# Linear attention, soft mixture and a wide layer in one program: weight tiles requested later, slot sums in another bank, and work moved between GpSimd and VectorE

## The chip, the cores and the metric

The program runs on one core of a Trainium2 chip. Times are microseconds on the device, of one execution. The kernel before takes 391.36 us, the median of three runs (391.15 to 392.89).

## The reference

Three layers follow each other. The first is a linear attention with decay, over batch 4, 8 heads, 768 positions and head size 48. A state of 48x48 per head is decayed by `w` at every position and takes up the outer product of key and value; the position's own product counts with the bonus `u` in place of 1:

```
cur = einsum('bhd,bhe->bhde', u * kt, vt)
y[:, :, t] = einsum('bhd,bhde->bhe', rt, state + cur)
state = w * state + einsum('bhd,bhe->bhde', kt, vt)
```

Its 3072x384 output `x` goes into a soft mixture of 8 experts with 4 slots each: `logits = x @ phi`, a softmax over the tokens makes each of the 32 slots' inputs (`d.T @ x`), each expert takes its 4 slots through `relu(s @ w1[e]) @ w2[e]`, and a softmax over the slots mixes the results back to tokens. The third layer is `g = max(0.01*h, h)` of `h = x @ w_in` and `g @ w_out`, with 2048 hidden columns. All is float32.

## The kernel before, in words

The attention is worked in 24 passes, called units in the code (`i`, 0 to 23): 6 chunks of 128 positions (`c`) times 4 pairs of heads (`k`, or `hp`), chunk by chunk. A pass needs two tiles from memory: `rkb` (r and k with the head dimension on the partitions, 128x1024 numbers, 512 KB) and `tk` (v, k and r with the tokens on the partitions, 128x1152, 576 KB). There are five buffers of each. SyncE issues all transfers in program order; in pass `i` it first requests that pass's weight tiles (the list `WST` says which pass each of the 22 tiles is requested in), then `rkb` and `tk` of unit `i+4`, whose buffers come free when TensorE has read those of unit `i-1`.

The order of instructions on every engine is that of the Python code. For one unit the steps are these. `scale` (line 303) multiplies r and k of `rkb` by powers of the decay, two instructions of 112x512: r on GpSimd, k on VectorE. The table of powers lies in SBUF (`ET`) and in PSUM (`ETp`). `bonus` (line 310) multiplies r by u and then by k in the token layout, two instructions of 128x384 on GpSimd (lines 314 and 317; for units 0 and 1 on VectorE). `diag` (line 319) sums that on VectorE into `Dg` and lets ScalarE write eight diagonal blocks into `base` (line 337). `keys` (line 342) scales the keys for the state. `scores` (line 355) are 8 products into the bank `A`; `keep` (line 365) copies their kept triangle from `A` into `base`, two VectorE instructions. `attend` (line 376) multiplies the state (line 391) and the values (line 399) into `Y`; `evac` copies `Y` to `xT` on ScalarE (line 432). `logits` (line 434) multiplies `xT` by phi, `tokens` transposes it, `update` makes the new state (`U`, then `St` on VectorE, line 421).

In pass `i` scale, bonus and diag are done for unit `i+2`, scores and keep for `i+1`, attend and update for `i`, logits and tokens for `i-1`. Once a chunk, one pass after its end (`k == 0`), `soft1` takes the maximum and the exponential of the chunk's logits. In the pass after that (`k == 1`: 5, 9, 13, 17, 21) `soft2` transposes them, `slots` (line 509) multiplies them with the tokens (`pS`), and `slots_add` adds the result to `acc` on VectorE (lines 523 and 526). `pS` has a buffer of the pool `psM`, which has two and which it shares with `U`, the token transposes `px` and the narrowing's `low`; so it takes the buffer that `U` of the same pass had, which is free when VectorE has read it. The logits of a chunk lie in a 2 KB bank of their own (`psL`, one buffer; 128 of its 512 columns are used).

Four of the weight tiles (`wir`, of `w_in`) are 64-bit floats and are narrowed to 32 bits between the passes, half a tile at a time, in the eight passes of the list `NARROW`: ScalarE makes one part one or two passes ahead (`narrow_a`, line 167), VectorE does three instructions of 128x384 at the end of the pass (lines 172, 178, 183). The weight pool `wp` has 18 buffers; tiles 18 to 21 of the list take the buffers of the narrowed tiles 0 to 3. Tiles 4 to 19 are `w1`; 20 and 21 are the first rows tiles of `w2`. The remaining rows of `w2` are requested after the passes, as buffers come free.

After the passes TensorE works nearly without a break: the experts' first product (`ph`, line 751), the second (`po`, line 794), the mixing weights' transposes, and then the wide layer (lines 959 and 1016) to the end.

Of the kernel before, what the change touches and what calls it, by code (L numbers as in the profile page):

```python
# [8 lines left out]
F32 = mybir.dt.float32  # L9
# [4 lines left out]
ALU = mybir.AluOpType  # L14
# [4 lines left out]
C = 128  # L19
NC = S // C  # L20
NP = H // 2
NU = NC * NP
DM = H * D
# [16 lines left out]
FILL_L = {3: 2}  # L40
WST = list(range(22))
NARROW = [5, 7, 9, 11, 13, 15, 17, 19]
WCH = 8
# [74 lines left out]
def chunked(ctx, tc, rk, tok, wT, urep, phi, w1, w2, win, wout, outT, dbg=None, check=False):  # L118
# [184 lines left out]
    def scale(i, eng=nc.gpsimd, part=(0, 1)):  # L303
        for x in part:
            t = rk_t[i][:, x]
            e = ETp[:R] if x and i else ET
            e = e[:, i % NP : i % NP + 1, :].broadcast_to([R, B, C])
            (nc.vector if x else eng).tensor_tensor(t, t, e, op=ALU.mult)  # L308

# [124 lines left out]
    def logits(i):  # L434
        c, hp = divmod(i, NP)
        if hp == 0:
            lw[c] = psL.tile([128, 4, C], F32, name=f"l{c}", tag="l")
            lps[c] = lw[c][:, 0]
        for b in range(B):
            nc.tensor.matmul(  # L440
                lps[c][32 * b : 32 * b + 32, :], phi_sb[:, hp, b % 2, :], xT[i][:, b, :],
                start=hp == 0, stop=hp == NP - 1, skip_group_check=True,
            )
# [65 lines left out]
    def slots(c, pS=None):  # L509
        if pS is None:  # L510
            pS = psM.tile([128, DM], F32, name=f"pS{c}", tag="m")
        for b in range(B):
# [51 lines left out]
    keys(0)  # L564
    powers(2)

    for i in range(NU):
# [15 lines left out]
        if i + 1 < NU:  # L583
            scores(i + 1)
            keep(i + 1)
        if i >= 1:
            logits(i - 1)
        if 2 <= i < NP:
            tokens(i - 2)(nc.scalar.copy)
        if i + 2 < NU:  # L590
            bonus(i + 2)
        attend(i)
        slot = bool(c) and k == 1
        if slot:
# [4 lines left out]
        if i < NP - 1:  # L599
            powers_t(i + 1)  # L600
            keys(i + 1)
        if i == 0:
            powers(3)
        if i == NP:
# [17 lines left out]
        if slot:  # L622
            pS = slots(c - 1)
        if i >= NP - 1:
            tok_copy(nc.scalar.copy)
        if slot:
            slots_add(c - 1, pS)
        if i in NARROW:
# [5 lines left out]
            narrow_d(wi[:, j, w], wirs[j], w, low)  # L634
        ahead = i + 1 + i % 2
        if ahead in NARROW and k > 1:
            j, x = divmod(NARROW.index(ahead), 2)
            w = slice(x * WCW // 2, (x + 1) * WCW // 2)
            narrow_a(wi[:, j, w], wirs[j], w)

    load_w2_unit(NLD - 1)
    m1, s1 = mst[:, NC - 1 : NC], sst[:, NC - 1 : NC]
    cb = cp.tile([128, 8], F32, name="cb")
# [547 lines left out]
```

## Time and profile before

| what | us |
|---|---|
| median of three runs | 391.36 |
| the profiled execution's own time | 391.55 |
| its span, from first to last instruction | 389.8 |
| busy: TensorE, VectorE, ScalarE, GpSimd | 369.3, 272.5, 234.1, 149.6 |
| the passes, to the first instruction of line 751 | 127.3 |

The span is 1.75 us shorter than the execution's own time; the rest lies before the first and after the last instruction. Busy time adds up over stages: for the passes, which end at 127 us, one reads the stretch from 0 to 127, and there what each engine waited for. "DVE" is VectorE, "ACT" ScalarE, "POOL" GpSimd, "PE" TensorE, "SPq" the queue of SyncE. In a row of the timeline the bracket at the end is the idle time of the engine ahead of the instruction and what ended it.

### The profile page before, as it was taken

The numbers are of one execution on the slowest core, as the hardware profiler recorded it, in microseconds if no ns is written. First come the engines' busy times: TensorE is split into PE (matmuls) and PEld (weight loads), VectorE is DVE, ScalarE is ACT, GpSimd is POOL, SyncE is SP. The second block draws the span as 40 slices with busy tenths as digits, with TensorE's granted clock in tenths as the row PEclk, the third lists the DMA queues.
The fourth block names the chain that finished last, engine by engine and source line by source line (L and its number), as shares of the span: only waits on it lengthen the run. The fifth ranks groups of instructions, "written<-read, shape, count | busy, mean of one in ns | idle before, by whom it ended". The sixth has DMA issues, their size and how long they took to land.

```text
span 389.8 us, 8335 instructions
## 1 busy us (share of the span) xinstructions
PE 369.3 (95%) x3162; PEld 282.7 (73%) x3162; DVE 272.5 (70%) x472; ACT 234.1 (60%) x542; POOL 149.6 (38%) x150
## 2 busy tenths in 40 slices
PE   6889898989999999899999999999999999999994
PEld 3567776767776345788888878888888888888883
DVE  6778787878785638667577755777765766586762
ACT  3378686969785214757676648667655455545440
POOL 4798998988641303155423332555200000000000
PEclk9999999999999999999999999999999999999998
DMA  7999999999998899400022220000000120021202
GB/s 250 407 419 414 415 413 418 416 416 417 414 386 297 286 392 419 184 2 0 0 83 82 81 82 0 0 3 1 1 3 0 72 91 0 1 105 59 81 3 88
DMA packets 21090, 70.16 MB, mean 180 GB/s; under 512 B 2240, under 2 KB 7344, under 8 KB 20912
## 3 DMA queue, kind: packets, MB, share of 16 engines
q1 hardware_dynamic: 21040, 69.53, 45.9%
q8 instruction: 27, 0.44, 0.5%
q14 instruction: 23, 0.19, 0.1%
HBM read 64.80 MB, written 4.72 MB: 178 GB/s over the span
## 4 chain that ended last, share of the span: by engine, by line
PE 69%; DVE 12%; ACT 7%; POOL 5%; issue 4%; DVEq 0%; POOLq 0%; ACTq 0%
PE o L1016 51%; PE h L959 6%; ACT base L337 6%; PE po L794 3%; DVE base L368 3%; PE ph L751 3%; DVE Dg L322 2%; DVE rkb L308 2%; POOL rkb L308 2%; POOL tk L314 1%; DVE low L178 1%; PE pS L515 1%; DVE low L172 1%; POOL tk L317 1%; POOL tk L349 1%
## 5 line engine op out<-in xcount | busy, mean ns | idle before, releaser
L973 ACT CAST gh<-t 128x512 fp32r<-128x512 f32 x94 | 58.4, 621 | 69.1 <-DVE t L969 61.5
L969 DVE TENSOR_TENSOR t<-t,h 128x512 f32<-128x512 f32 (+1 forms) x97 | 65.7, 678 | 26.0 <-ACT t L965 25.1
L1016 PE MATMUL o<-gh,woh 128*128 128x512 f32 x279 | 80.4, 395 | 0.0
L1016 PE MATMUL o<-gl,woh 128*128 128x512 f32 x279 | 80.2, 394 | 0.0
L1016 PE MATMUL o<-gh,wol 128*128 128x512 f32 x279 | 80.2, 394 | 0.0
L978 DVE TENSOR_TENSOR gl<-t,gh 128x512 fp32r<-128x512 f32 x71 | 50.2, 708 | 40.7 <-ACT gh L973 39.9
L965 ACT ACTIVATE t<-h 128x512 f32<-128x512 f32 (+1 forms) x97 | 57.4, 593 | 13.7 <-PE h L959 13.1
L1016 PEld LDWEIGHTS o<-gh,woh 128*128 128x128 f32 x279 | 52.5, 188 | 12.3 <-DVE sum L1087 0.2
L1016 PEld LDWEIGHTS o<-gl,woh 128*128 128x128 f32 x279 | 52.5, 188 | 12.1
L1016 PEld LDWEIGHTS o<-gh,wol 128*128 128x128 f32 x279 | 52.3, 188 | 12.0 <-issue 0.4
L337 ACT ACTIVATE base<-anti,Dg 128x128 f32<-128x128 f32 x176 | 53.9, 389 | 11.5 <-DVE Dg L322 10.7
L978 POOL TENSOR_TENSOR gl<-t,gh 128x512 fp32r<-128x512 f32 x23 | 34.2, 1488 | 51.8 <-ACT gh L973 48.5
L368 DVE COPY_PREDICATED base<-mask,A 128x512 f32<-128x512 int32 x48 | 34.2, 735 | 11.1 <-ACT base L337 10.4
L959 PE MATMUL h<-cT,Gs 128*128 128x512 f32 (+1 forms) x97 | 37.7, 394 | 1.4 <-ACT Gs L927 1.4
L360 PE MATMUL A<-rkb 48*128 48x128 f32 x384 | 28.0, 284 | 5.3 <-DVE base L368 4.2
L360 PEld LDWEIGHTS A<-rkb 48*128 48x128 f32 x384 | 23.7, 188 | 11.7 <-issue 3.5
L308 POOL TENSOR_TENSOR rkb<-rkb,ETw 112x512 f32<-112x512 f32 x23 | 27.9, 1212 | 5.2 <-DMA rkb<-in_rk_dram 5.2
L399 PE MATMUL Y<-base,tk 128*48 128x128 f32 x376 | 25.5, 277 | 0.0
L314 POOL TENSOR_TENSOR tk<-tk,u_sb 128x384 f32<-128x384 f32 x22 | 22.1, 1002 | 4.1 <-DMA tk<-in_tok_dram 3.0
L399 PEld LDWEIGHTS Y<-base,tk 128*48 128x48 f32 x376 | 19.4, 122 | 4.9 <-issue 3.0
L317 POOL TENSOR_TENSOR tk<-tk 128x384 f32<-128x384 f32 x22 | 22.1, 1003 | 1.7
L861 POOL TENSOR_TENSOR wol<-wor,woh 128x384 fp32r<-128x384 f32 x8 | 9.5, 1197 | 33.4 <-ACT woh L860 33.4
(199 smaller groups left out, 476.2 us busy)
## 6 DMA issues: line engine op xcount, KB each, us to landing
w<-in_w_dram SPq DMA_DIRECT2D x24, 768.0 KB, 10.9
tk<-in_tok_dram SPq DMA_DIRECT2D x23, 576.0 KB, 9.9
rkb<-in_rk_dram SPq DMA_DIRECT2D x24, 512.0 KB, 9.7
wir<-in_win_dram SPq DMA_DIRECT2D x8, 768.0 KB, 13.5
out_dram<-sum SPq DMA_DIRECT2D x17, 256.0 KB, 2.1
wor<-in_wout_dram SPq DMA_DIRECT2D x4, 768.0 KB, 9.6
wir<-in_wout_dram SPq DMA_DIRECT2D x4, 768.0 KB, 4.2
w2t<-in_w_dram SPq DMA_DIRECT2D x4, 576.0 KB, 6.5
```

The lines of the kernel that those rows point to most:

```text
L308: (nc.vector if x else eng).tensor_tensor(t, t, e, op=ALU.mult)
L314: eng.tensor_tensor(rr, rr, u_sb[:, hp : hp + 1, :].broadcast_to([128, B, 2 * D]), op=ALU.mult)
L337: nc.scalar.activation(base[i][:, h, b, :], anti, AF.Copy, scale=Dg[i][:, h * B + b : h * B + b + 1])
L360: nc.tensor.matmul(a[:, h, b, :], rk_t[i][p0 : p0 + D, 1, b, :], rk_t[i][p0 : p0 + D, 0, b, :], start=True, stop=True,)
L368: nc.vector.copy_predicated(base[i][:, :, 2 * j : 2 * j + 2, :], mask.unsqueeze(1).unsqueeze(1).broadcast_to([128, 2, 2, C]), a[:, :, 2 * ...
L399: nc.tensor.matmul(ys[r][g : g + D, j, :], v[:, b, D * h : D * h + D], base[i][:, h, b, :], start=c == 0, stop=True, skip_group_check=True,)
L959: nc.tensor.matmul(t, Gs[f // 8][:, f % 8 * 128 : f % 8 * 128 + 128], cT[blk // 3][:, blk % 3 * TB + c.start : blk % 3 * TB + c.stop], sta ...
L965: nc.scalar.mul(tt[n][:, c], t, 0.01)
L969: nc.vector.tensor_tensor(tt[n][:, c], tt[n][:, c], h, op=ALU.max)
L973: nc.scalar.copy(gh[n][:, c], tt[n][:, c])
L978: eng.tensor_tensor(gl[n][:, c], tt[n][:, c], gh[n][:, c].bitcast(F32), op=ALU.subtract)
L1016: nc.tensor.matmul(os[m][:, c], w[j][:, k, m * 128 : (m + 1) * 128], g[n][:, c], start=k == 0 and w is woh and g is gh and c.start == 0, s ...
```

## The change

Six edits, all in the passes.

- `WST`: the first weight tile is requested in pass 2 and not in pass 0, one a pass to pass 18, none in pass 19, two each in 20 and 21, and the last after the passes. The last rows and tokens (unit 23) are requested in pass 19; 17 tiles stand ahead of them and 5 behind, before it was 20 and 2.
- `slots` writes into columns 128 to 511 of the bank in which the next chunk's logits stand, and no longer into a buffer of `psM`. The tile of that bank is made in `slots`; the chunk's first logits, `logits(i-1)` of the pass with `k == 1`, move from the middle of the pass to right behind the slots' product.
- `NARROW`: the narrowings of passes 13 and 17 are now in passes 20 and 22. The new table `NARROW_A` says in which pass ScalarE makes its part.
- `SCALE_V`: r of the units 9, 13, 17 and 21 is scaled on VectorE (in passes 7, 11, 15 and 19), from the table in PSUM.
- The bonus of unit 2, in pass 0, is on VectorE.
- `powers(3)`, the table of powers of the last pair of heads (three VectorE and three ScalarE instructions), stands ahead of pass 0 and no longer at its end.

```
-WST = list(range(22))
-NARROW = [5, 7, 9, 11, 13, 15, 17, 19]
+WST = [*range(2, 19), 20, 20, 21, 21, NU]
+NARROW = [5, 7, 9, 11, 15, 19, 20, 22]
+NARROW_A = {3: 5, 6: 7, 7: 9, 10: 11, 14: 15, 18: 19, 19: 20, 21: 22}
+SCALE_V = (9, 13, 17, 21)
...
-            e = ETp[:R] if x and i else ET
+            e = ETp[:R] if (x or i in SCALE_V) and i else ET
...
-            (nc.vector if x else eng).tensor_tensor(t, t, e, op=ALU.mult)
+            (nc.vector if x or i in SCALE_V else eng).tensor_tensor(t, t, e, op=ALU.mult)
...
-            lw[c] = psL.tile([128, 4, C], F32, name=f"l{c}", tag="l")
+            if c == 0:
+                lw[c] = psL.tile([128, 4, C], F32, name=f"l{c}", tag="l")
...
-            pS = psM.tile([128, DM], F32, name=f"pS{c}", tag="m")
+            lw[c + 1] = psL.tile([128, 4, C], F32, name=f"l{c + 1}", tag="l")
+            pS = lw[c + 1][:, 1:4].rearrange("p a t -> p (a t)")
...
     powers(2)
+    powers(3)
...
-        if i >= 1:
+        slot = bool(c) and k == 1
+        if i >= 1 and not slot:
             logits(i - 1)
...
-            bonus(i + 2)
+            bonus(i + 2, nc.gpsimd if i else nc.vector)
...
-        if i == 0:
-            powers(3)
...
         if slot:
             pS = slots(c - 1)
+            logits(i - 1)
...
-        ahead = i + 1 + i % 2
-        if ahead in NARROW and k > 1:
-            j, x = divmod(NARROW.index(ahead), 2)
+        if i in NARROW_A:
+            j, x = divmod(NARROW.index(NARROW_A[i]), 2)
...
     load_w2_unit(NLD - 1)
+    load_weights(len(WST) - 1)
```

What the two programs have on VectorE around pass 0, before and then with the change. `ETw` is the table of powers, `rkb` the scaling of unit 2, `base` the `keep` of unit 1, `tk` the bonus and `Dg` the sum of unit 2; the line numbers of the changed kernel are two to four higher.

```order
L274 SCALAR_TENSOR_TENSOR ETw<-W_139,ETw,zp 112x63
L308 TENSOR_TENSOR rkb_111<-rkb_111,ETp 112x512
L368 COPY_PREDICATED base_197<-mask,A_213 128x2x256 x2
L274 SCALAR_TENSOR_TENSOR ETw<-W_139,zp 112x64
L286 RECIPROCAL ETw<-ETw 112x1
L274 SCALAR_TENSOR_TENSOR ETw<-W_139,ETw,zp 112x63
L322 TENSOR_REDUCE Dg_247<-tk_131 128x4x2
L419 COPY St<-U_258 112x192
```

```order
L276 SCALAR_TENSOR_TENSOR ETw<-W_139,ETw,zp 112x63
L276 SCALAR_TENSOR_TENSOR ETw<-W_139,zp 112x64
L288 RECIPROCAL ETw<-ETw 112x1
L276 SCALAR_TENSOR_TENSOR ETw<-W_139,ETw,zp 112x63
L310 TENSOR_TENSOR rkb_111<-rkb_111,ETp 112x512
L370 COPY_PREDICATED base_197<-mask,A_217 128x2x256 x2
L316 TENSOR_TENSOR tk_131<-tk_131,u_sb 128x384
L319 TENSOR_TENSOR tk_131<-tk_131 128x384
L324 TENSOR_REDUCE Dg_245<-tk_131 128x4x2
L421 COPY St<-U_256 112x192
```

The three instructions of `powers(3)` moved ahead of the scaling, and the two of the bonus, which GpSimd had, came in ahead of the sum.

VectorE in passes 13 to 15, before and then with the change: `acc` adds the slots' sums, `low` and `wi` are the narrowing, `rkb` the scaling of units 15, 16 and 17, `base` the `keep`.

```order
L421 SCALAR_TENSOR_TENSOR St<-St,W_139,U_1233 112x192
L526 SCALAR_TENSOR_TENSOR acc<-acc,st_1138,pS_1248 128x384
L528 SCALAR_TENSOR_TENSOR sst<-sst,st_1138 128x1
L172 TENSOR_SCALAR low_1259<-wir_328 128x384
L178 SCALAR_TENSOR_TENSOR low_1259<-wi,low_1259 128x384
L183 SCALAR_TENSOR_TENSOR wi<-wir_328,low_1259 128x384
L308 TENSOR_TENSOR rkb_110<-rkb_110,ETp 112x512
L368 COPY_PREDICATED base_1223<-mask,A_1270 128x2x256 x2
L322 TENSOR_REDUCE Dg_1305<-tk_1096 128x4x2
L421 SCALAR_TENSOR_TENSOR St<-St,W_139,U_1317 112x192
L308 TENSOR_TENSOR rkb_111<-rkb_111,ETp 112x512
L368 COPY_PREDICATED base_1307<-mask,A_1341 128x2x256 x2
```

```order
L423 SCALAR_TENSOR_TENSOR St<-St,W_139,U_1221 112x192
L530 SCALAR_TENSOR_TENSOR acc<-acc,st_1131,l_1236 128x384
L532 SCALAR_TENSOR_TENSOR sst<-sst,st_1131 128x1
L310 TENSOR_TENSOR rkb_110<-rkb_110,ETp 112x512
L370 COPY_PREDICATED base_1211<-mask,A_1258 128x2x256 x2
L324 TENSOR_REDUCE Dg_1293<-tk_1089 128x4x2
L423 SCALAR_TENSOR_TENSOR St<-St,W_139,U_1305 112x192
L310 TENSOR_TENSOR rkb_111<-rkb_111,ETp 112x512 x2
L370 COPY_PREDICATED base_1295<-mask,A_1329 128x2x256 x2
```

The narrowing of pass 13 is gone from behind `acc`, and in pass 15 the scaling is two instructions in place of one.

TensorE in pass 17, before and then with the change: `A` the scores of unit 18, then 19, `l` the logits, `Y` the attention and the transposes of `soft2`, `pS` the slots' sums, which are `l` from columns 128 on with the change; the state's products `U` are left out.

```order
L360 MATMUL A_1495<-rkb_112 128x128 x8
L440 MATMUL l_1506<-xT_1449,phi_sb 32x128 x4
L391 MATMUL Y<-rkb_111,St 48x128 x8
L399 MATMUL Y<-base_1378,tk_1175 48x128 x8
...
L448 MATMUL px_1558<-ident,xT_1449 128x112 x4
L515 MATMUL pS_1563<-xtok_1255,dl_1531 32x384
L515 MATMUL pS_1563<-xtok_1255,dl_1531 32x4x48 x2
...
L360 MATMUL A_1585<-rkb_113 128x128 x8
```

```order
L362 MATMUL A_1482<-rkb_112 128x128 x8
L393 MATMUL Y<-rkb_111,St 48x128 x8
L401 MATMUL Y<-base_1366,tk_1168 48x128 x8
...
L451 MATMUL px_1540<-ident,xT_1436 128x112 x4
L519 MATMUL l_1545<-xtok_1247,dl_1513 32x384
L519 MATMUL l_1545<-xtok_1247,dl_1513 32x4x48 x2
...
L443 MATMUL l_1545<-xT_1436,phi_sb 32x128 x4
L362 MATMUL A_1567<-rkb_113 128x128 x8
```

The logits of unit 16 moved from ahead of the attention to between the slots' sums and the scores of unit 19.

## Rows read from the trace of the kernel before

**Rows 1.** Windows: us; busy us by engine (instructions); clock; DMA share, GB/s; 45 to 72.
```profile
45.00:72.00 27.00, 24.61 (x450) 19.73 (x452) 22.84 (x43) 22.19 (x69) 24.59 (x25) 1.00 1.02 416
```

**Rows 2.** Line 317 (bonus): who waited for it, us in total, times.
```profile
  DVE Dg L322: 3.1, 5
```

**Rows 3.** Timeline 13 to 39: start, us, engine, line [idle before <-releaser].
```profile
13.45 0.69 DVE L308 TENSOR_TENSOR rkb<-rkb,ETp 112x512 f32<-112x512 f32 x1 [0.43 <-ACT ETp L282]
...
15.29 0.26 DVE L274 TENSOR_TENSOR_SCAN ETw<-W,zp 112x64 f32<-112x64 f32 x1
...
15.79 0.34 DVE L274 TENSOR_TENSOR_SCAN ETw<-W,ETw,zp 112x63 f32<-112x63 f32 x1
...
17.49 0.56 DVE L322 TENSOR_REDUCE Dg<-tk 128x8 f32<-128x384 f32 x1 [1.36 <-POOL tk L317]
...
26.44 0.87 DVE L349 TENSOR_TENSOR tk<-tk,KH 128x384 f32<-128x384 f32 x1
...
31.97 1.00 POOL L314 TENSOR_TENSOR tk<-tk,u_sb 128x384 f32<-128x384 f32 x1 [0.61 <-DMA tk<-in_tok_dram]
...
34.96 0.55 DVE L349 TENSOR_TENSOR tk<-tk,KH 128x384 f32<-128x384 f32 x1
...
35.01 1.64 POOL L308 TENSOR_TENSOR rkb<-rkb,ETw 112x512 f32<-112x512 f32 x1 [0.81 <-DMA rkb<-in_rk_dram]
```

**Rows 4.** Waits, 45 to 112: us in total, times, longest us.
```profile
DVE base L368 <- ACT base L337: 6.2, 14, 0.5
...
PE pS L515 <- DVE St L421: 1.9, 3, 0.6
```

**Rows 5.** Timeline of passes 13 to 15, 78 to 87.
```profile
78.46 0.86 PE L515 MATMUL pS<-xtok,dl 128*32 128x384 f32 x12 [0.65 <-DVE St L421]
...
79.39 0.61 DVE L526 SCALAR_TENSOR_TENSOR acc<-acc,st,pS 128x384 f32<-128x384 f32 x1 [1.08 <-PE pS L515]
...
80.34 0.43 PE L440 MATMUL l<-xT,phi_sb 112*32 112x128 f32 x8
...
80.38 0.55 DVE L172 TENSOR_SCALAR low<-wir 128x384 int32<-128x384 uint32 x1
...
82.03 0.68 DVE L308 TENSOR_TENSOR rkb<-rkb,ETp 112x512 f32<-112x512 f32 x1
...
84.28 1.16 PE L360 MATMUL A<-rkb 48*128 48x128 f32 x16 [0.94 <-DVE base L368]
...
84.45 2.45 ACT L337 ACTIVATE base<-anti,Dg 128x128 f32<-128x128 f32 x8 [1.44 <-DVE Dg L322]
...
85.76 0.74 DVE L368 COPY_PREDICATED base<-mask,A 128x512 f32<-128x512 int32 x1 [0.43 <-ACT base L337]
...
86.93 0.75 DVE L368 COPY_PREDICATED base<-mask,A 128x512 f32<-128x512 int32 x1 [0.44 <-ACT base L337]
```

**Rows 6.** Timeline of passes 18 to 20, 102 to 107.
```profile
102.56 1.00 POOL L317 TENSOR_TENSOR tk<-tk 128x384 f32<-128x384 f32 x1
...
103.26 2.45 ACT L337 ACTIVATE base<-anti,Dg 128x128 f32<-128x128 f32 x8 [1.11 <-DVE Dg L322]
...
105.98 0.58 ACT L168 ACTIVATE wi<-wir 128x384 f32<-128x384 f32 x1
...
106.38 0.54 DVE L322 TENSOR_REDUCE Dg<-tk 128x8 f32<-128x384 f32 x1
```

**Rows 7.** Timeline of passes 22 and 23, 119 to 122.
```profile
119.09 0.59 ACT L432 COPY xT<-Y 112x512 f32<-112x512 f32 x1 [0.44 <-PE Y L399]
...
121.80 0.42 DVE L430 COPY xT<-ylast 112x256 f32<-112x256 f32 x1 [1.90 <-PE ylast L399]
```

**Rows 8.** Transfers issued at 102.05 (last token tile): KB, us to landing.
```profile
tk<-in_tok_dram SPq DMA_DIRECT2D x1, 576.0 KB, 8.3
```

**Rows 9.** Transfers issued about 139.1 (last row tile of w2).
```profile
w<-in_w_dram SPq DMA_DIRECT2D x2, 768.0 KB, 11.0
```

**Rows 10.** TensorE's timeline: the second half of the experts' output product.
```profile
147.83 5.37 PE L794 MATMUL po<-w,hTm 128*32 128x384 f32 x64
```

More of the change, by code (lines that the diff above doesn't have):

```diff
@@ L590, in chunked @@
         if i + 2 < NU:
-            bonus(i + 2)
+            bonus(i + 2, nc.gpsimd if i else nc.vector)
         attend(i)
-        slot = bool(c) and k == 1
         if slot:
```

## The prediction

> **What bounds the kernel now.** The chain of waits, read from its end, is TensorE almost alone from 127 us on; the change touches nothing there but the arrival of weights. The question is how fast the 24 passes run. The windows by stage come next: between 45 and 72 us all four engines are busy for 82 to 91% and the transfers all the time, at 416 GB/s [rows 1]. Shares do not decide between five candidates; the waits do.
>
> Up to 39 us GpSimd sets the pace: VectorE's sum for the diagonal waits for its bonus five times, 3.1 us together [rows 2], the first time 1.36 [rows 3]. GpSimd in turn waits 0.61 and 0.81 us for tiles [rows 3]. After that nobody waits for GpSimd: in pass 19 its bonus for unit 21 ends at 103.56, and VectorE takes it up at 106.38 [rows 6]. From 45 to 112 the path goes to and fro: VectorE waits 14 times for ScalarE's blocks, 6.2 us together, and TensorE's slots' sums wait three times 0.6 us for VectorE [rows 4]. Passes 13 to 15 show the loop [rows 5]: `acc` starts at 79.39, after 1.08 us idle, the narrowing holds VectorE from 80.38 to 82.03, the diagonal's sum comes late, so ScalarE has waited 1.44 us at 84.45 and TensorE's scores 0.94 at 84.28; in the pass after, VectorE waits 0.43 and 0.44 for ScalarE. The transfers are full, but their data come well ahead of use: they cap the gain and do not set the pace.
>
> **The change part by part.** Times are those of the profiled execution; what I subtract from it I subtract from the median too, 0.19 us below it.
>
> *The start.* GpSimd loses the two instructions of unit 2's bonus, 1.0 us each as all of that line [rows 3], and is 2.0 us earlier from then on. VectorE gains them: 0.55 us each alone, 0.87 beside GpSimd, by the two rows of line 349, which has the same shape; at 34.96 GpSimd stood still, at 26.44 it worked [rows 3]. `powers(3)`, from 15.29 to 16.13, moves ahead of a scaling that waited 0.43 for ScalarE [rows 3], so 0.41 of its 0.84 shows. VectorE was free at 15.29; the diagonal's sum of unit 2 now starts at 15.29 + 0.41 + 1.1 to 1.74, which is 16.8 to 17.45 in place of 17.49. I take 17.25, a gain of 0.25, nearer the contended end since GpSimd has no gap there. The other four waits, 3.1 - 1.36 = 1.74 us, go, since GpSimd is 2.0 us ahead and the two waits for tiles vanish too (below). Sum: -2.0, bounds -2.4 and -1.7.
>
> The Trainium skill (SBUF — State Buffer, Who interferes with whom) says that a VectorE instruction with two SBUF inputs shares a read port with GpSimd and that the loser blocks, while one with an input in PSUM does not collide. The pair 0.55 and 0.87 agrees. By that rule alone the start would give -1.8, and without it -2.4.
>
> *Scaling r of four units on VectorE.* Each is 0.68 us, as its k [rows 5]. They stand in passes 7, 11, 15 and 19 ahead of the keep that waits 0.43 + 0.44 = 0.87 us for ScalarE [rows 5], and the end of the second wait is set by ScalarE's eight blocks, not by VectorE. So 0 is taken; uncovered it is 4 x 0.68 = 2.7. GpSimd's 4 x 1.2 us less are worth nothing, since nobody waits for it then; below nothing the edit cannot go.
>
> *Slots' sums in the logits' bank.* In the passes 5, 9, 13 and 17 the product no longer waits 0.65 us for VectorE to empty `U` [rows 5]. But the logits of unit i-1, 0.43 us [rows 5], now stand directly behind it and write the same tile. VectorE's `acc` waits for the last writer of the tile it reads, so it starts 0.65 - 0.43 = 0.2 us earlier, not 0.65. On TensorE the logits are only moved. Passes 5 and 9: -0.4 together, bounds 0 and -1.3.
>
> The Trainium skill (PSUM — Partial Sum Buffer, PSUM bank collisions raise a hardware error) says that a matmul and a VectorE read must not touch one bank and the same partitions at a time, and asks to guard by bank, not by address. No row here has both in one bank. By the rule `acc` must wait for the logits, the -0.4 taken; without it the two passes would give -1.3.
>
> *Narrowing out of passes 13 and 17.* VectorE loses 80.38 to 82.03 = 1.65 us [rows 5], and with the 0.2 reaches the diagonal's sum 1.85 earlier. It cannot use all: ScalarE's blocks could start 1.44 earlier, plus 0.2 for TensorE; TensorE's scores 0.94 + 0.2 earlier, then TensorE itself runs without a gap. Between 1.15 and 1.65 I take 1.4. For pass 17 ScalarE's wait was 1.11 [rows 6], so at most 1.3, and in the same ratio at least 0.9; I take 1.1. Sum -2.5, bounds -2.05 and -2.95.
>
> *Narrowing in passes 20 and 22, and the tail.* In pass 20 VectorE's 1.65 us stand ahead of the keep of unit 22, which waits for ScalarE as in pass 15, 0.87 us; up to 0.8 shows at the diagonal of unit 23, and ScalarE has slack of its own there. ScalarE's 0.58 us for the narrowing [rows 6] then stand ahead of the copy at 119.09, which had 0.44 us of idle time [rows 7]. In pass 21 the moved logits add 0.43 to TensorE, which has no gap there. These lie side by side, the largest decides, and I take +0.7. The narrowing of pass 22 fits into VectorE's wait of 1.90 at 121.80 [rows 7]. Bounds 0 and +3.9, if both narrowings and ScalarE's part lay open (2 x 1.65 + 0.58).
>
> *Transfers.* A weight tile is 786 KB (128x1536 numbers), at 416 GB/s 1.9 us. Loads from unit 6 on have two tiles fewer ahead, 3.8 us, those of unit 23 three, 5.7 us. That removes the waits of 0.61 and 0.81. At unit 21 there were 2.8 us to spare; with 3.8 the passes may gain 6.6 before data hold them. The price comes after: the last tokens land 5.7 us before 102.05 + 8.3 = 110.35 [rows 8], at 104.65; then follow 13 tiles to the last rows of w2, five pieces of 983 KB and one of 1,376 KB, 16.5 MB or 39.7 us: 144.3. TensorE needs that tile in the last eighth of its row, at 147.83 + 7/8 x 5.37 = 152.5 [rows 10], less the gain: 148.3. Hidden, with 4 us to spare; before it landed at 139.1 + 11.0 = 150.1 [rows 9].
>
> Sum: -2.0 - 0.4 - 2.5 + 0.7 = -4.2. Span 385.6, this execution 387.35, median **387.2**.
>
> **The rivals.**
>
> *The holes in the queue stay holes.* Tiles for later units are requested only when buffers come free. If the two skipped requests leave the transfers idle instead of moving the rows up, unit 21 has its old 2.8 us to spare, and the passes gain 2.8 - 0.7 = 2.1: 389.3. For it: the requests wait for TensorE. Against it: the tiles wanted in those passes took long behind others, GpSimd waiting for two of them [rows 3].
>
> *Weights late.* From 110.35 to 150.1 before, 14.1 MB came: 356 GB/s, not 416, as requests waited for buffers. At that rate 16.5 MB take 46.4 us from 104.65, to 151.0, 2.7 after the need: gain 1.5, 389.9. For it: that rate is measured; against it: the extra tiles are requested early and fill the gaps.
>
> *VectorE's added work lies open (slower).* The path of passes 7 to 23 runs through VectorE. If the blocks come earlier too and its waits of 0.43 vanish, the four scalings cost 2.7, and the moved narrowings 3.9 where they arrive; against 2.0, 0.4 and 2.5 gained, +1.7: 393.1. It decides where VectorE's wait ahead of the keep in passes 7, 11, 15, 19 is gone and ScalarE waits for it instead. Against it: 14 such waits [rows 4].
>
> *More than I take.* The bonus uncontended (0.4), the upper bounds for passes 13 and 17 (0.45), and a free tail (0.7): -5.7, 385.7.
>
> **How the numbers follow.** The forecast 0.57 (its own range 386.2 to 388.4), the open holes 0.12, late weights 0.10, VectorE open 0.08, more 0.13. The range 385.2 to 390.3 takes in all but VectorE's case and the ends. About what a measurement can tell from no change is 0.5%, 1.96 us: faster is below 389.4. That holds for the forecast, for more, and for nearly half of the first two rivals: 0.78. Within it, 0.14; slower by more, 0.08.
>
> **What would show it.** In the profile after: VectorE's diagonal sums no longer waiting for GpSimd before 39 us; the slots' sums starting without a wait for VectorE, and `acc` still idle 0.85 us before it; keeps of passes 7, 11, 15, 19 without their first wait and with the second; the last token tile landing near 104.7; TensorE's first instruction of the experts 4 us earlier, at 123, and no wait for a transfer in the row of 64. I am wrong if the experts start after 125, or start early and then wait for weights.

## The result, and the profile after

The changed kernel took **387.02 us** (median of 4 runs, 386.33 to 388.15) beside 391.81 us for the kernel before on the same chip (4 runs, 391.15 to 392.89): a ratio of 0.9878, 95% interval 0.9841 to 0.9915. The forecast was 387.2. The number fits better than its terms: the start lost time instead of gaining it, and other places, some of them not the change's, gained what it lost. Below, a pair of numbers in brackets behind a time is its ratio to the kernel before and the 95% interval.

First the page of the profile after: its span, the chain by engine, and the last row of part 2 (GB/s in 40 slices):

```profile
span 384.7 us, 8325 instructions
...
PE 76%; DVE 8%; ACT 5%; POOL 5%; issue 2%; DMA 2%; SPq 1%; POOLq 0%; DVEq 0%; ACTq 0%
...
GB/s 262 401 412 412 407 417 415 418 414 415 399 412 382 371 402 425 84 2 0 0 85 82 83 83 0 1 2 1 2 2 0 82 83 0 1 133 33 82 3 89
```

The same two rows of the page before:

```profile
PE 69%; DVE 12%; ACT 7%; POOL 5%; issue 4%; DVEq 0%; POOLq 0%; ACTq 0%
...
GB/s 250 407 419 414 415 413 418 416 416 417 414 386 297 286 392 419 184 2 0 0 83 82 81 82 0 0 3 1 1 3 0 72 91 0 1 105 59 81 3 88
```

The span is 5.1 us shorter than 389.8. VectorE's share of the chain fell from 12 to 8%, TensorE's rose from 69 to 76%. The dip of the transfers to 297 and 286 GB/s in slices 13 and 14 of before is gone (382 and 371).

Where in the passes the time went is read from two milestones of each pass: the start of TensorE's 16 scores, and of VectorE's sum for the diagonal. This table is worked out from the timelines of TensorE and VectorE; the two last columns are experiments (below) in which two small operations of VectorE have another form:

| stretch (us) | before | after | before, small form | after, small form |
|---|---|---|---|---|
| diagonal sum of unit 1 to scores of 6 | 22.78 | 23.34 | 22.75 | 23.54 |
| scores 6 to 7 (pass 5, slots) | 6.07 | 5.20 | 5.60 | 5.20 |
| scores 7 to 11 (pass 9, slots) | 19.49 | 17.92 | 18.55 | 17.93 |
| scores 11 to 14 | 13.17 | 13.36 | 12.87 | 12.87 |
| scores 14 to 16 (pass 13) | 11.08 | 9.41 | 10.49 | 9.31 |
| scores 16 to 18 | 8.13 | 8.04 | 8.16 | 8.04 |
| scores 18 to 20 (pass 17) | 10.65 | 9.85 | 10.50 | 9.27 |
| scores 20 to the experts | 24.28 | 24.36 | 24.28 | 24.36 |
| sum | 115.65 | 111.48 | 113.20 | 110.52 |

TensorE's first matmul of the experts, before and after:

```profile
127.34 7.93 PE L751 MATMUL ph<-w,slT 128*32 128x512 f32 x72
```

```profile
123.40 7.93 PE L755 MATMUL ph<-w,slT 128*32 128x512 f32 x72
```

It started 3.94 us earlier. The table has 4.17, because the diagonal sum of unit 1 itself came 0.23 later. That moment lies between 11.69 and 12.75 in the profiled executions of this study, depending on when the first tiles land; for that reason the stretches begin behind it. The rest of the 5.1 us, 1.1, lies behind 127 us, in code that the change does not touch. From the experts' start to the end took 262.5 us before, 261.3 after, and 260.6 to 263.8 in the other profiled executions in which no matmul waited for weights, so I do not put this 1.1 down to the change.

The start after, VectorE and GpSimd, in order of time (start us, us, engine, line, tiles, idle before):

```profile
14.44 0.69 DVE L310 TENSOR_TENSOR rkb<-rkb,ETp 112x512 f32<-112x512 f32 x1 [0.43 <-ACT ETp L284]
...
16.27 0.75 DVE L316 TENSOR_TENSOR tk<-tk,u_sb 128x384 f32<-128x384 f32 x1
17.05 1.52 DVE L319 TENSOR_TENSOR tk<-tk 128x384 f32<-128x384 f32 x1
18.60 0.56 DVE L324 TENSOR_REDUCE Dg<-tk 128x8 f32<-128x384 f32 x1
...
26.70 0.56 DVE L324 TENSOR_REDUCE Dg<-tk 128x8 f32<-128x384 f32 x1 [0.54 <-POOL tk L319]
```

```profile
16.56 1.59 POOL L310 TENSOR_TENSOR rkb<-rkb,ETw 112x512 f32<-112x512 f32 x1
...
22.38 1.00 POOL L351 TENSOR_TENSOR tk<-tk,KH 128x384 f32<-128x384 f32 x1 [1.88 <-ACT KH L298]
```

These answer to [rows 3]. The sum for unit 2 no longer waits for GpSimd, but it starts at 18.60, 1.11 later than the 17.49 of before. VectorE's bonus took 2.33 us from 16.27 to 18.60, not 1.1 to 1.74: its second product took 1.52 beside GpSimd's scaling, and ended 0.42 behind it (18.57 and 18.15). And GpSimd, two instructions lighter, stood 1.88 us before its keys of unit 2, waiting for a copy of ScalarE.

Passes 13 to 15 after, VectorE and TensorE's scores, which answer to [rows 5]:

```profile
77.25 0.61 DVE L530 SCALAR_TENSOR_TENSOR acc<-acc,st,l 128x384 f32<-128x384 f32 x1 [0.57 <-PE l L443]
...
77.91 0.68 DVE L310 TENSOR_TENSOR rkb<-rkb,ETp 112x512 f32<-112x512 f32 x1
```

```profile
77.13 1.16 PE L362 MATMUL A<-rkb 48*128 48x128 f32 x16
...
81.15 1.16 PE L362 MATMUL A<-rkb 48*128 48x128 f32 x16
...
85.17 1.05 PE L362 MATMUL A<-rkb 48*128 48x128 f32 x14
```

VectorE goes from `acc` to the scaling without the narrowing, `acc` waits 0.57 for the logits instead of 1.08 for the product, and the scores follow each other by 4.02 us without a wait. From 77.13 to 89.19, where the scores of unit 18 begin, TensorE is busy without a gap. Here (us of the stretch, busy time by engine, clock, DMA share, GB/s):

```profile
77.13:89.19 12.06, 12.06 (x233) 9.96 (x229) 10.91 (x21) 10.09 (x31) 9.53 (x10) 1.00 1.02 415
```

### The profile page after: what moved, and what is told of

Same layout as the page of the kernel before. It is cut to its first block, busy times and chain, and to the rows that moved or that the text cites. A ratio compares the mean times of both kernels' runs of the same rounds, so it can differ in the third digit from the quotient of the medians.

```text
span 384.7 us, 8325 instructions
## 1 busy us (share of the span) xinstructions
PE 367.6 (96%) x3162; PEld 283.4 (74%) x3162; DVE 275.9 (72%) x478; ACT 233.3 (61%) x542; POOL 144.1 (37%) x144
## 4 chain that ended last, share of the span: by engine, by line
PE 76%; DVE 8%; ACT 5%; POOL 5%; issue 2%; DMA 2%; SPq 1%; POOLq 0%; DVEq 0%; ACTq 0%
PE o L1020 51%; PE h L963 6%; ACT base L339 3%; PE po L798 3%; PE ph L755 3%; PE A L362 2%; PE Y L401 2%; DVE base L370 2%; DMA tk<-in_tok_dram 2%; POOL tk L316 1%; POOL rkb L310 1%; POOL tk L319 1%; PE Y L393 1%; PE px L451 1%; DVE Dg L324 1%
## 5 line engine op out<-in xcount | busy, mean ns | idle before, releaser
L969 ACT ACTIVATE t<-h 128x512 f32<-128x512 f32 (+1 forms) x97 | 57.4, 592 | 12.5 <-PE h L963 11.2
L1020 PEld LDWEIGHTS o<-gl,woh 128*128 128x128 f32 x279 | 52.5, 188 | 11.7
L1020 PEld LDWEIGHTS o<-gh,wol 128*128 128x128 f32 x279 | 52.2, 188 | 11.7 <-issue 0.4
L310 POOL TENSOR_TENSOR rkb<-rkb,ETw 112x512 f32<-112x512 f32 x19 | 23.4, 1234 | 1.9 <-DMA rkb<-in_rk_dram 1.9
L963 PEld LDWEIGHTS h<-cT,Gs 128*128 128x128 f32 x97 | 18.0, 188 | 5.6 <-ACT Gs L931 1.8
```

Of the source, the lines that this page charges most:

```text
L310: (nc.vector if x or i in SCALE_V else eng).tensor_tensor(t, t, e, op=ALU.mult)
L963: nc.tensor.matmul(t, Gs[f // 8][:, f % 8 * 128 : f % 8 * 128 + 128], cT[blk // 3][:, blk % 3 * TB + c.start : blk % 3 * TB + c.stop], sta ...
L969: nc.scalar.mul(tt[n][:, c], t, 0.01)
L1020: nc.tensor.matmul(os[m][:, c], w[j][:, k, m * 128 : (m + 1) * 128], g[n][:, c], start=k == 0 and w is woh and g is gh and c.start == 0, s ...
```

## The experiments

All times stand beside the kernel before run on the same chip, whose medians were 391.5 to 391.8 us. Since the runs of one kernel scatter by 1.5 to 4.5 us, the milestones of the traces decide between theories where fractions of a us are in question.

**Undoing the start.** In the changed kernel:

```
-    powers(3)                     # ahead of the loop
+        if i == 0: powers(3)      # in pass 0
-            bonus(i + 2, nc.gpsimd if i else nc.vector)
+            bonus(i + 2)
```

> The changed kernel with the start as before: unit 2's bonus on GpSimd, powers(3) at the end of pass 0. Theory (the new start costs): VectorE's diagonal sum of unit 2 comes back from 18.6 to about 17.5, TensorE's scores of unit 7 from 40.46 to 39.6-39.8, the experts' first matmul from 123.40 to about 122.6, time about 0.8 us below the changed kernel, 386.2. Rival A (the delay of the start is taken up again later, since TensorE or the transfers set the pace of the last passes): unit 7 at 39.7, but the experts still at 123.2 to 123.5, time 387.0. Rival B (my forecast: the new start gains): diagonal sum of unit 2 no earlier, scores of unit 7 later than 41, time 389.

387.52 us (0.9884, 0.9839 to 0.9930). The diagonal sum of unit 2 came back to 17.60, the scores of unit 7 started at 39.76, 0.70 earlier, and the experts at 122.97, 0.43 earlier. From the sum of unit 1 to the scores of 6 it is 22.77, the 22.78 of before. The new start does cost time, and in this execution some of it is taken up later; the median does not resolve so little. My forecast for the start is refuted. Both of its edits are undone here together, and no run has either alone.

**The start alone**, the same lines put into the kernel before:

> The kernel before with the new start alone (unit 2's bonus on VectorE, powers(3) ahead of the loop). Theory (the new start costs): diagonal sum of unit 2 from 17.49 to about 18.6, scores of unit 7 from 40.54 to 41.2-41.4, experts from 127.34 to 127.9-128.2, time about 392.4. Rival A (taken up later): unit 7 late, experts at 127.3, time 391.8. Rival B (my forecast for the start): experts at 125.3, time 389.8.

392.02 us (1.0013, 0.9992 to 1.0033): no change. The sum of unit 2 stood at 18.50 and the scores of unit 7 at 41.52, 0.98 late; the experts started at 127.38, not late at all. By the scores of unit 11 (60.09 against 60.03) the delay was gone: the running maximum of pass 8, 1.18 us before, took 0.26 here (two small operations, below).

**The slots' sums alone** in the kernel before (`pS = lw[c + 1][:, 1:4]`, and `logits(i - 1)` behind `slots(c - 1)`):

> The kernel before with the slots' sums in the logits' bank and the logits moved behind them, nothing else. Theory (in the changed kernel acc waited 0.57 to 0.68 in place of 1.08 in each of the passes 5, 9, 13, 17): 0.4 to 0.5 a pass, the experts about 1.6 to 2.0 earlier, 125.3 to 125.7, time 389.9 to 390.2; the 128x1 maximum of pass 8 may stay at 1.18 or not, which would be 1.0 more. Rival (my forecast): 0.2 a pass, 0.8 together, experts at 126.5, time 391.0.

389.10 us (0.9931, 0.9905 to 0.9958). The scores of unit 21 were 2.55 us earlier than before, those of unit 23 only 0.50, the experts 0.50. Between the scores of 20 and 23 the trace lost 2.0 us (14.9 in place of 12.9). The longest waits from 100 to 116 us (us in total, times, longest):

```profile
POOL rkb L308 <- DMA rkb<-in_rk_dram: 3.0, 3, 1.0
```

A gain of 2.5 us was there by unit 21, of which 0.92 is the running maximum of pass 8 (0.26 us here, 1.18 before). In this execution, with 391.06 us one of the two slowest of eight, most of it was lost again at units 21 to 23.

**The narrowing's units alone** (`NARROW`, `NARROW_A` and its test) in the kernel before:

> The kernel before with the narrowing at the new units alone. Theory (my forecast's step, without the 0.2 of the slots): passes 13 and 17 gain 1.2 and 0.9 to 1.1, the passes 20 to 22 give back 0 to 0.1, experts at 125.0 to 125.4, time 389.5 to 389.9. Rival (the gain of 1.67 and 0.80 us seen in the changed kernel came with the earlier slots' sums, and alone VectorE's acc, which still waits 1.08, holds TensorE): 0.8 a pass, experts at 125.8, time 390.3. Rival (the tail gives back 0.7, as forecast): experts at 126, time 390.4.

395.92 us (1.0101, 1.0040 to 1.0162): slower, against all three expectations. The experts started 1.02 earlier, at 126.32, and then TensorE waited in the wide row of the experts' output. SyncE's waits ahead of its transfers, in the whole span, and that row:

```profile
SPq L548 <- DVE wi L184: 17.6, 2, 11.7
```

```profile
148.22 4.08 PE L794 MATMUL po<-w,hTm 128*32 128x384 f32 x48
153.30 0.85 PE L794 MATMUL po<-w,hTm 128*32 128x384 f32 x8 [1.00 <-DMA w<-in_w_dram]
155.26 0.85 PE L794 MATMUL po<-w,hTm 128*32 128x384 f32 x8 [1.11 <-DMA w<-in_w_dram]
```

The buffers of the last two raw tiles of `win` come free only once units 19 and 22 have narrowed them, and the loads of w2 that take them stood, at units 20 and 21 as before, ahead of everything else in the queue, the longest 11.7 us. Later requests were put off with them. In all, TensorE's weight loads of that row waited 5.9 us for `w`, five times. The rival of the prediction that weights come late came true here. In the passes the narrowing gave 1.01 us in pass 14 and 0.64 in pass 18, by TensorE's scores (table further below).

**Narrowing with the new units of the weight tiles** (`WST` added):

> The kernel before with the new units of the weight tiles and of the narrowing, without the rest. Theory (with the narrowing alone the loads of w2 stood behind wi's buffers in SP's queue, 11.7 us; the weight tiles' new units take just that away): passes 13 and 17 gain 1.0 to 1.2 each as with the narrowing alone, no wait of TensorE for w2, experts at 125.0 to 126.3, time 388.9 to 390.3. Rival (w2 is late with the new units too, since less time is left): TensorE still waits 1 to 3 us for w, time 391 or more. Rival (my forecast's sizes): passes 13 and 17 -2.5, tail +0.7, experts at 125.5.

388.93 us (0.9928, 0.9887 to 0.9968). TensorE had no wait for w2; the experts started at 124.93. Scores 14 to 16 took 10.29 us and 18 to 20 took 9.96, that is 0.79 and 0.69 less than before, and 20 to the experts 24.23. Each of the two gains is below the 1.0 to 1.2 expected. The tail gives nothing back, and the pair of edits belongs together. No run has the table of weight tiles alone; here it is what lets the narrowing move.

**Slots' sums with the new units of the weight tiles:**

> The kernel before with the new units of the weight tiles and the slots' sums in the logits' bank, narrowing and start as before. Theory (with the slots alone 2.5 us were gained by the scores of unit 21, and 2.0 of it lost in passes 21 and 22, where GpSimd waited 1.0 three times for r; two weight tiles fewer ahead of those loads take that away): the scores of unit 23 about 2.5 us earlier than before, experts at 124.5 to 125.0, time 388.5 to 389.3. Rival (the loss in passes 21 and 22 is not the transfers'): experts at 126.8 as with the slots alone, time 390.5 to 391.

390.05 us (0.9962, 0.9932 to 0.9992); nine executions lay between 388.2 and 392.6, the tenth took 395.2 at a granted clock of 0.984. In the trace the scores of unit 23 were 2.0 us earlier (113.92) and the experts as much, 125.34: from 20 to 23 it took 13.1 us, so the hold of the run with the slots alone is gone. But passes 13 and 14 gained nothing (11.04 us), since VectorE's running maximum (`mst`) and running sum (`sst`) took 0.71 and 0.86 there (0.50 and 0.53 before).

**Two small operations.** In the trace of before one row had been overlooked. In pass 8 the running maximum, 128x1 numbers, took 1.18 us, beside GpSimd's scaling (start us, us):

```profile
53.27 1.27 POOL L308 TENSOR_TENSOR rkb<-rkb,ETw 112x512 f32<-112x512 f32 x1
...
53.38 1.18 DVE L476 TENSOR_TENSOR mst<-mst,st 128x1 f32<-128x1 f32 x1
```

After, the same operation came when one instruction of GpSimd ended (53.23) and before the next began:

```profile
52.23 1.00 POOL L316 TENSOR_TENSOR tk<-tk,u_sb 128x384 f32<-128x384 f32 x1
...
53.16 0.15 DVE L479 TENSOR_TENSOR mst<-mst,st 128x1 f32<-128x1 f32 x1
...
53.30 1.00 POOL L319 TENSOR_TENSOR tk<-tk 128x384 f32<-128x384 f32 x1
```

In the kernel before:

```
-  nc.vector.tensor_tensor(mst_c, mst_c1, st0, op=ALU.max)
+  nc.vector.tensor_scalar(mst_c, mst_c1, st0, -3.0e38, op0=ALU.max, op1=ALU.max)
-  nc.vector.scalar_tensor_tensor(sst_c, sst_c1, st3, st2, op0=ALU.mult, op1=ALU.add)
+  nc.vector.tensor_scalar(sst_c, sst_c1, st3, st2, op0=ALU.mult, op1=ALU.add)
```

> The kernel before with two of VectorE's 128x1 operations in the form tensor_scalar (one tensor operand and the rest as per-row scalars): the running maximum and the running sum, four of each in the passes. Theory (with two tensors from SBUF the 128x1 maximum stands still while GpSimd's instruction beside it runs: 1.18 us in pass 8, and 0.4 to 0.6 in others): each takes 0.15 to 0.22, pass 8 is 1.0 shorter, scores of unit 11 at 59.0, experts 0.8 to 1.3 earlier, 126.0 to 126.5, time 390.6. Rival A (the operand form has no part in it): still 0.5 to 1.2. Rival B (short now, but VectorE's slack takes it): experts at 127.3, time 391.6.

389.42 us (0.9929, 0.9896 to 0.9963), and experts at 125.05, 2.29 earlier: more than expected. Every maximum took 0.20 and every sum 0.27:

```profile
53.03 0.20 DVE L476 TENSOR_SCALAR mst<-mst,st 128x1 f32<-128x1 f32 x1
...
59.42 0.27 DVE L530 TENSOR_SCALAR sst<-sst,st 128x1 f32<-128x1 f32 x1
```

Before, they had taken 1.18, 0.50, 0.43, 0.25 and 0.57, 0.53, 0.21, 0.21.

**GpSimd's lead.** The changed kernel with `powers(3)` back in pass 0, and ScalarE's copies KH earlier:

```
-            powers_t(i + 1)
+            for x in ((1, 2), (3,), ())[i]: powers_t(x)
```

> The changed kernel with powers(3) back at the end of pass 0 (unit 2's bonus stays on VectorE) and ScalarE's copies KH for units 2 and 3 a pass earlier. Theory (GpSimd's lead is lost where its keys of unit 2 wait 1.88 for KH, which ScalarE makes behind unit 2's blocks; powers(3) cost 1.0 us of the start): diagonal sum of unit 2 at 17.5 to 17.7 in place of 18.60; GpSimd's keys of unit 2 without that wait, VectorE's sums of units 4 and 5 without a wait for GpSimd, scores of unit 7 at 38.6 to 39.6 in place of 40.46; experts 0.4 to 1.0 before 123.40, time 386.0 to 386.6. Rival (the pace of the start is the ring of ScalarE's blocks, VectorE and TensorE, not GpSimd): the waits for GpSimd go, the scores of unit 7 stay at 39.7 to 40.4.

387.14 us (0.9865, 0.9817 to 0.9913), the experts at 123.96. The first tiles landed late in this execution (sum of unit 1 at 12.69); from that sum to the scores of 6 it is 22.67 us, 0.67 less than in the changed kernel. The wait for KH is gone, and another has taken its place:

```profile
19.25 1.29 POOL L310 TENSOR_TENSOR rkb<-rkb,ETw 112x512 f32<-112x512 f32 x1 [1.86 <-DVE ETw L276]
```

```profile
16.30 1.50 DVE L316 TENSOR_TENSOR tk<-tk,u_sb 128x384 f32<-128x384 f32 x1
17.84 0.56 DVE L319 TENSOR_TENSOR tk<-tk 128x384 f32<-128x384 f32 x1
18.31 0.28 DVE L276 TENSOR_TENSOR_SCAN ETw<-W,zp 112x64 f32<-112x64 f32 x1
...
19.09 0.53 DVE L324 TENSOR_REDUCE Dg<-tk 128x8 f32<-128x384 f32 x1
```

GpSimd now waits for `powers(3)`, which stands behind the bonus on VectorE. With the bonus there, VectorE has no gap left in which `powers(3)` is free. The expectation of 17.5 for the sum of unit 2 failed; the waits of units 4 and 5 shrank only to 0.17 and 0.49.

The traces still decide between theory and rival. The start has two parts, with VectorE's waits for GpSimd in the second (us):

| stretch | before | after | this run |
|---|---|---|---|
| sum of unit 1 to sum of unit 2 | 5.80 | 6.68 | 6.40 |
| sum of unit 2 to scores of 6 | 16.98 | 16.66 | 16.27 |
| waits for GpSimd, units 3 to 5 | 1.37 | 1.09 | 0.66 |

What these waits lose, 0.28 and 0.71, the second part gains (0.32 and 0.71). So GpSimd does set the pace there, as the forecast had it; the time is lost ahead of the sum of unit 2. The run with the start alone falls out of this row (17.43, with waits of 1.24): there a product of VectorE for the keys took 1.92 us, 0.96 before.

**The change on the small form.** The changed kernel with the two small operations as above, and three variants, all on one chip.

> The changed kernel with the running maximum and sum as tensor_scalar. Theory (these 128x1 operations stood beside GpSimd in the changed kernel too: 0.83 in pass 16, 0.72 in pass 9, 0.35 in pass 12, together 1.3 more than at their shortest): experts 0.5 to 1.3 before 123.40, and against the kernel before with the same edit (125.05) the change is worth 2.2 to 2.7, less than the 3.94 that the two traces show, since 1.0 of that was the maximum of pass 8 falling clear of GpSimd by chance. Rival (VectorE's 1.3 is hidden since TensorE sets the pace there): experts at 123.2 to 123.5, and the change worth 1.6 to 1.9 on this base.

385.71 us (0.9849, 0.9825 to 0.9874), experts at 123.27. The first tiles landed late (sum of unit 1 at 12.75); from there on it is 0.96 less than the changed kernel. The last two columns of the table compare the change free of those operations: 113.20 against 110.52, so **2.68 us** are the change's own, near the upper end of what was expected, and 1.49 of the 4.17 are not in it: 0.79 behind the scores of unit 7 (the small operations), 0.47 in pass 5 and 0.23 ahead of the scores of unit 6. The medians, each against the kernel before on its chip, put the change on the small form at 0.9929 - 0.9849 = 0.8%, 3.1 us; their intervals allow 1.5 to 4.8.

The same with the old start:

> The same with the start as before too (unit 2's bonus on GpSimd, powers(3) at the end of pass 0). Theory (the new start costs 0.8 by unit 7, of which 0.4 lasts): experts 0.4 to 0.8 before those of the kernel with the new start and the same small operations, 121.8 to 122.5; time 385.3 to 386.0, below the changed kernel. Rival (TensorE or the transfers take the whole up): experts within 0.2 of it.

385.56 us (0.9865, 0.9840 to 0.9889), experts at 121.91, the earliest of all. From the sum of unit 1 to the scores of 6 it takes 22.76 instead of 23.54, and nothing of that 0.78 is taken up later: 81.76 against 81.78 us from the scores of 7 to the experts.

The same with the logits ahead of the attention again, in the shared bank (`lw[c]` taken in `logits`, no test of `slot`):

> The same with the logits of the slots' passes ahead of the attention again, in the shared bank, so that VectorE's acc waits for the slots' sums alone. Theory (acc waits for the last writer of its tile, the logits behind the sums, 0.35 to 0.43): acc idle 0.2 instead of 0.57 in passes 5 to 17; passes 5 and 9, where a narrowing follows, gain 0.3 to 0.4 each, experts 0.5 to 0.8 before the run without this edit, time 384.8 to 385.3. Rival A (TensorE is without a gap there, and the logits ahead delay the attention by the same 0.43): experts the same within 0.2. Rival B (acc does not start earlier): acc idle 0.57 as before.

386.49 us (0.9869, 0.9849 to 0.9889), experts at 122.45. Rows of pass 9, first of the run above (old start, logits behind), then with the logits ahead:

```profile
58.19 0.61 DVE L532 SCALAR_TENSOR_TENSOR acc<-acc,st,l 128x384 f32<-128x384 f32 x1 [0.57 <-PE l L443]
```

```profile
58.68 0.61 DVE L530 SCALAR_TENSOR_TENSOR acc<-acc,st,l 128x384 f32<-128x384 f32 x1 [0.64 <-PE l L519]
```

`acc` waits for the product alone now, and no less: TensorE, with the logits ahead, comes to the product later. Scores 7 to experts 81.93, against 81.76. That is rival A.

The changed kernel on the small form, without the scalings of r on VectorE (`SCALE_V = ()`):

> The changed kernel with the small operations as tensor_scalar and the four scalings of r back on GpSimd. Theory (my forecast's step: on VectorE they lie in its wait for ScalarE's blocks): experts within 0.3 of the kernel that differs from it only in these. Rival A (they lie open on VectorE, up to 4 x 0.68): experts 0.5 to 2.7 earlier. Rival B (GpSimd, whose tiles now come late, needs the relief): experts 0.5 to 1.5 later.

385.39 us (0.9869, 0.9838 to 0.9900); scores 7 to experts 81.92 against 81.78. The four scalings are worth 0.1, within what these traces can tell from nothing.

The three versions at 385.4 to 385.7 us stand below both kernels. Against the kernel before that is certain; against the changed kernel the intervals of the ratios overlap, and only the milestones (0.8 to 1.75 us, by the table's measure) speak for it.

## Why the prediction was right, and where it was wrong

**The start: wrong in sign.** Forecast -2.0, measured +0.56 in the two traces, +0.79 on the small form, and undone by putting it back. Three steps failed. "So 0.41 of its 0.84 shows": with `powers(3)` ahead, the scaling again waited 0.43 for ScalarE's copy, at 14.44 instead of 13.45, as it now waits for the later of two copies into one tile; of the 0.99, 0.23 were there at the sum of unit 1, and 0.76 showed. "VectorE gains them: 0.55 us each alone, 0.87 beside GpSimd": the 0.87 was a row in which the two happened to overlap in part, and 0.75 + 1.52 came. In both rows VectorE's product ended 0.42 behind the GpSimd instruction that was running when it started: 27.31 against 26.89 in the row of before, 18.57 against 18.15 after. So its length depends on how much of GpSimd's instruction is left, and 0.87 was no upper bound. GpSimd beside the 0.87:

```profile
25.89 1.00 POOL L349 TENSOR_TENSOR tk<-tk,KH 128x384 f32<-128x384 f32 x1
```

Last, "2.0 us earlier from then on": GpSimd's own list holds the keys of unit 2, which need ScalarE's copy behind the blocks of unit 2, which need VectorE's sum of unit 2. A lead on GpSimd ends at the first instruction that depends on the engine which took over its work. The experiment with the earlier copies shows the next such instruction behind it. Of the four later waits for GpSimd two went, and two stayed at 0.54 and 0.55; that GpSimd's two waits for tiles would go was right.

**Scaling r: right.** Forecast 0, measured 0.1. The sign named there, keeps without the first wait and with the second, came in passes 7 and 11; in 15 and 19 both waits are gone. Keeps of passes 11 and 15 after:

```profile
65.13 0.73 DVE L370 COPY_PREDICATED base<-mask,A 128x512 f32<-128x512 int32 x1
66.22 0.76 DVE L370 COPY_PREDICATED base<-mask,A 128x512 f32<-128x512 int32 x1 [0.36 <-ACT base L339]
...
82.42 1.58 DVE L370 COPY_PREDICATED base<-mask,A 128x512 f32<-128x512 int32 x2
```

In all four passes the scores follow each other by 4.02 or 4.03 us, with TensorE busy throughout, so VectorE's extra 0.68 does not show.

**Slots' sums: right in mechanism, mis-sized.** Forecast -0.2 a pass. Pass 5 gave -0.40 on the small form, and the stretch with pass 9 -0.62. The steps were 0.65 - 0.43 and "On TensorE the logits are only moved", at nothing. Pass 9 on the small form, of before and then of after:

```profile
57.96 0.86 PE L517 MATMUL pS<-xtok,dl 128*32 128x384 f32 x12 [0.39 <-DVE St L421]
...
58.89 0.61 DVE L528 SCALAR_TENSOR_TENSOR acc<-acc,st,pS 128x384 f32<-128x384 f32 x1 [1.08 <-PE pS L517]
```

```profile
58.41 0.86 PE L521 MATMUL l<-xtok,dl 128*32 128x384 f32 x12
58.58 0.41 DVE L423 SCALAR_TENSOR_TENSOR St<-St,W,U 112x192 f32<-112x192 f32 x1
...
59.08 0.41 PE L443 MATMUL l<-xT,phi_sb 112*32 112x128 f32 x8
...
59.55 0.62 DVE L532 SCALAR_TENSOR_TENSOR acc<-acc,st,l 128x384 f32<-128x384 f32 x1 [0.56 <-PE l L443]
```

The product starts while VectorE is still at `St`, and the logits start at 59.08, before the product's 0.86 are over: both are done 1.08 us after the product's start, so the logits cost 0.22 and not 0.43. And ahead of the product they are missing: counted from the scores of unit 10 (52.96 and 54.13) the product starts at 5.00 before and 4.28 after. About half of these 0.72 is the wait for VectorE, 0.39; the other half is the logits, since `U` already starts 0.36 earlier (3.41 and 3.05). So the scores of unit 11 come 0.72 - 0.22 = 0.50 earlier, and `acc` is idle 0.52 less. The wait on the logits itself came as forecast. The Trainium skill (PSUM — Partial Sum Buffer, PSUM bank collisions raise a hardware error) asks that a matmul and a VectorE read never touch one bank and the same partitions at the same time, and to guard by bank; the trace has that order, `acc` behind the logits of the same bank in all five passes with slots' sums.

**Narrowing out of passes 13 and 17: right in mechanism, priced too high.** Forecast -1.4 and -1.1, 0.2 of the slots' gain included in each; measured -1.18 and -1.23 on the small form, again with the slots' gain. The experiments tell the two edits apart: the slots' sums shorten the pass in which they stand, the narrowing the pass after it. From scores to scores, us:

| scores | before | slots alone | narrowing alone | before, small form | after, small form |
|---|---|---|---|---|---|
| 14 to 15 (pass 13) | 6.05 | 5.31 | 6.05 | 5.79 | 5.29 |
| 15 to 16 (pass 14) | 5.03 | 4.69 | 4.02 | 4.70 | 4.02 |
| 18 to 19 (pass 17) | 5.99 | 5.68 | 6.49 | 5.80 | 5.25 |
| 19 to 20 (pass 18) | 4.66 | 4.63 | 4.02 | 4.70 | 4.02 |

The 6.49 has a running maximum of 0.98 us in it. On the small form the narrowing is worth 0.68 in each place, not 1.2 and 0.9, and the slots' sums 0.50 and 0.55, not 0.2: two errors of opposite sign. What ends the narrowing's gain is the case named in the forecast, TensorE without a gap, 4.02 us a pass. So TensorE's own wait, 0.94 in [rows 5] and 0.61 on the small form, was about all that could go; the step that took 1.4 above the lower bound of 1.15, for ScalarE's 1.44, failed.

**The tail: too dear.** Forecast +0.7, measured +0.08. VectorE's narrowing in pass 20 and ScalarE's share lay beside TensorE, which sets the pace there after the change.

**Transfers: hidden, but not with 4 us to spare.** The last tokens were asked for at 98.67 and took 5.6 us: 104.3, forecast 104.65. The last rows of w2 were asked for at 135.68 and took 12.5, so they landed at 148.2 and not at 144.3. The need, forecast for 148.3, was at 147.9: TensorE's weight load for these rows waited 0.29 us for them.

```profile
148.20 0.36 PEld L798 LDWEIGHTS po<-w,hTm 128*32 128x32 f32 x8 [0.29 <-DMA w<-in_w_dram]
```

So nothing was to spare. The step that failed took 16.5 MB at 416 GB/s behind the last tokens; from 104.3 to 148.2 the trace moved 17.4 MB at 395 GB/s. SyncE's requests waited for buffers that TensorE frees (5.1 us for the experts' transposes alone), which was left out; how much of the 3.9 us is due to that is not shown. The rate by which the rival priced late weights, 14.1 MB at 356 GB/s, reads 13.7 MB at 344 GB/s in the trace of before.

**What the forecast did not hold: luck.** Of the difference between the two traces 0.79 us are where VectorE's 128x1 operations fell beside GpSimd, 0.23 are in the start, and 0.47 are pass 5. There VectorE's sum at 38.73 waited 0.36 for GpSimd in the trace of before, behind the tile at 35.01 [rows 3]. The small form of before has such a tile wait too (0.50) without the loss, and the changed kernel has none; whether the 0.47 belong to the change, no run shows. Another 1.1 lies behind 127 us. With -2.68 the median would be about 388.7, with the 0.47 as well about 388.2, of 391.36. That 387.02 was measured beside 387.2 is luck: the start was forecast 2.8 us too well and the other terms 1.3 us too cautiously, and the remaining 1.5 came from outside these terms.

## What to carry over

Before an engine is called ahead, read its own list on to the next instruction that waits for the engine which took over the work; the lead ends there. A duration taken from a row in which two engines overlapped in part is no bound for a full overlap. And where edits share a queue's buffers (here the narrowing's units and the loads behind them), price them as a pair: alone one of them cost 4 us. A wait that one edit shortens is worth no more than the gap it leaves on the engine that then runs without a break.

## What was not expected of the hardware

A VectorE operation on 128x1 numbers with two tensors took from 0.15 to 1.18 us, by how much was left of the GpSimd instruction that was running when it started; the 1.18 ended with GpSimd's 1.27 us instruction (54.56 and 54.54). In all runs, each of these operations in passes 8 to 21 that took 0.25 us or more ended within 0.03 us of the end of such an instruction. With one tensor operand and the rest as per-row scalars it took 0.20 or 0.27 each time. A larger product can lose to two instructions of GpSimd in a row: the keys of unit 5, in the run with the start alone, started at 31.63 beside one and ended at 33.55, 0.42 behind the next.

```profile
31.08 1.09 POOL L308 TENSOR_TENSOR rkb<-rkb,ETw 112x512 f32<-112x512 f32 x1
...
31.63 1.92 DVE L349 TENSOR_TENSOR tk<-tk,KH 128x384 f32<-128x384 f32 x1
...
32.13 1.00 POOL L314 TENSOR_TENSOR tk<-tk,u_sb 128x384 f32<-128x384 f32 x1
```

The Trainium skill (SBUF — State Buffer, Who interferes with whom) has the rule: the port is an exclusive lock, and a VectorE instruction with two inputs from SBUF contends for it. The traces agree. The loss is thus set by GpSimd's instruction and not by the size of VectorE's: by the two forms eight small operations cost the kernel before 1.95 us from the scores of unit 7 to the experts (86.80 against 84.85).
